# x tiles 2-3 by DMA transpose on the ACT ring, all other loads in order on the SP ring, eight f tiles for tiles 0-1 first

## The chip, the cores and the metric

The kernel runs on one core of one Trainium2 chip. The metric is the device time of one execution in microseconds (us), the median over several executions. TensorE (PE) does the matmuls, VectorE (DVE) and ScalarE (ACT) move and activate what comes out of PSUM, and the SyncE (SP) and ACT sequencers ask for DMA transfers. Each of these two sequencers has a ring of its own, and both rings are served by the same 16 DMA engines. In the profile the SP ring is queue q1 and the ACT ring is q10.

Measured time before: 105.89 us (median of 6 runs in the rounds with the change).

## The reference

```python
# x: (1, 2048, 512)  w1: (512, 1792)  b1: (1792)  w2: (1792, 512), all bf16
h = einsum("bsd,df->bsf", x, w1) + b1
act = h * tanh(softplus(h))              # Mish
out = einsum("bsf,fd->bsd", act, w2)
```

The contraction of the first product runs over D, so x has to arrive with D on the partitions: it must be transposed.

## The kernel before

The 2048 rows of x are worked in four blocks of 512. For each block the 14 "f tiles" of h (128 columns of w1 each) are made by four matmuls of 512 columns (`mm1`), passed through Mish on ACT, and multiplied with w2 (`mm2`). Blocks 1 to 3 get x by DMA transpose. Block 0 cannot wait for that: its four x tiles of 128 rows are loaded plainly and transposed by TensorE.

```python
# loads of before, in order of issue (F0 = 4: f tiles 0-3 come first)
t_xa  = load(sp,  x tile 0)                    # 128 KB
t_w1k = load(act, w1 rows k 0-1, f 0-3)        # 256 KB
t_xb  = load(sp,  x tile 1)
t_w1k+= load(act, w1 rows k 2-3, f 0-3)        # "w1's lower half"
t_xc  = load(sp,  x tiles 2-3)
t_b1  = load(act, b1)
load(sp, w1 f 4-7); load(sp, w1 f 8-13); load(sp, w2)       # 512, 768, 1792 KB
for s in 1..3: load(sp, xT block s, x block s, transpose=True)
... # cut; what PE does in the head:
part_T([0], t_xa)                  # 4 transposes on PE, copies on DVE and ACT
first_mm1([0], by_k(0, 1))
part_T([1], t_xb)
first_mm1([1], by_k(0, 1)); first_mm1([0, 1], by_k(2))
part_T([2, 3], t_xc)               # 8 transposes on PE
first_mm1([0, 1], by_k(3))
first_mm1([2, 3], ...)             # f 0-3 are done for block 0
... # cut: b1 is transposed, Mish of f 0-3
for t in range(F0, FT): mm1(t)     # f 4-13, 512 columns at a time
```

(The first block above is shortened; arguments stand for the slices.)

## Time and profile before

| | before |
|---|---|
| median time | 105.89 us |
| span of the profiled run | 103.9 us |
| PE busy | 97% |
| first full `mm1` (f tile 4) starts | 8.83 us |
| `mm2` of block 0 starts | 17.25 us |

The page of before says what bounds it. The first line gives busy time and share of the span; the rows of digits give busy tenths in 40 slices of 2.6 us; the last two lines are the chain of waits by engine and by line.

```profile
PE 101.1 (97%) x513; PEld 50.0 (48%) x522; DVE 13.0 (12%) x25; ACT 40.4 (39%) x63; POOL 0.6 (1%) x6
...
PE   8999999999999999999999999999999999999992
...
PEclk9999999999999999999999999999999999999999
...
PE 97%; issue 1%; DVE 0%
PE ps L206 46%; PE ps L180 43%; PE ps L151 4%; PE ps L119 2%; PE ps L133 1%; DVE o_sb L210 0%; DVE warm L115 0%; PE ps L226 0%
```

TensorE is the bound from end to end. Only its first 9 us hold anything but full matmuls. The timeline of PE shows them (start, length, what, count, and in brackets the idle time before and what ended it):

```profile
3.15 1.03 PE L151 MATMUL ps<-xT,w_sb 128*128 128x128 bf16 x8
3.98 0.63 PE L133 MATMUL ps<-ident,x_nat 128*128 128x128 bf16 x4
4.61 1.32 PE L151 MATMUL ps<-xT,w_sb 128*128 128x128 bf16 x12
5.77 0.61 PE L133 MATMUL ps<-ident,x_nat 128*128 128x128 bf16 x8
6.22 2.35 PE L151 MATMUL ps<-xT,w_sb 128*128 128x256 bf16 x20
8.50 0.18 PE L226 MATMUL ps<-ident,b_nat 14*128 14x14 bf16 x1
8.83 8.58 PE L180 MATMUL ps<-xT,w_sb 128*128 128x512 bf16 x39 [0.16 <-issue]
17.25 2.97 PE L206 MATMUL ps<-w_sb,a_sb 128*128 128x512 bf16 x12
```

The eight transposes of tiles 2-3 are the line at 5.77; the next work starts 0.45 us later. That is what the change wants to save. In the instructions of this stretch, 128-column matmuls start 107 ns apart until 5.2 us and 56 ns apart afterwards: the TensorE clock is halved until then.

The DMA view of before gives each issue with its size and the time from issue to landing. The two first pieces of w1 go on the ACT ring; the second of them, issued at 0.58 us, lands at 4.76. The transposes are those of blocks 1 to 3.

```profile
w_sb<-in_w_dram SPq DMA_DIRECT2D x1, 1792.0 KB, 12.7
...
w_sb<-in_w_dram ACTq DMA_DIRECT2D x2, 256.0 KB, 3.6
...
xT<-in_x_dram SPq DMA_TRANSPOSE x3, 5.5
```

### The profile page before, as it was taken

Reading aid. Unit: us, or ns where it says so; the run is one execution under the profiler, and the core shown is the slowest. Engines: PE = TensorE matmul, PEld = TensorE weight load, DVE = VectorE, ACT = ScalarE, POOL = GpSimd, SP = SyncE. Lnnn points to the kernel's source line nnn. Section 1 sums busy time; section 2 is a strip of 40 time slices with the busy share of each in tenths; the row PEclk is TensorE's granted clock in tenths of the full one; section 3 lists DMA queues with packets and bytes.
Section 4 is the critical chain, followed back from the end, with each engine's and each line's share of the span. In section 5 each row is a group of like instructions: output and inputs, shape, how many; then the busy total and the mean of one; then the engine's idle time right before and its main releaser. Section 6 shows DMA issues by size and latency. Waiting matters only on the chain.

```text
span 103.9 us, 1168 instructions
## 1 busy us (share of the span) xinstructions
PE 101.1 (97%) x513; PEld 50.0 (48%) x522; DVE 13.0 (12%) x25; ACT 40.4 (39%) x63; POOL 0.6 (1%) x6
## 2 busy tenths in 40 slices
PE   8999999999999999999999999999999999999992
PEld 7895444444444444444444444444444444444462
DVE  0310000112220000022220000022112000011223
ACT  2525997000027777200007777500005777700000
POOL 2000000000000000000000000000000000000000
PEclk9999999999999999999999999999999999999999
DMA  5999996951101000010111000001111000001111
GB/s 169 294 349 376 349 187 149 260 146 50 50 7 43 0 6 0 0 50 14 37 50 50 0 3 6 0 0 50 50 50 50 0 0 0 0 6 50 50 50 51
DMA packets 12561, 7.94 MB, mean 76 GB/s; under 512 B 6796, under 2 KB 12428, under 8 KB 12556
## 3 DMA queue, kind: packets, MB, share of 16 engines
q1 hardware_dynamic: 11984, 7.34, 26.5%
q10 hardware_dynamic: 572, 0.53, 1.5%
q8 instruction: 4, 0.07, 0.3%
q14 instruction: 1, 0.01, 0.0%
HBM read 4.20 MB, written 2.10 MB: 61 GB/s over the span
## 4 chain that ended last, share of the span: by engine, by line
PE 97%; issue 1%; DVE 0%
PE ps L206 46%; PE ps L180 43%; PE ps L151 4%; PE ps L119 2%; PE ps L133 1%; DVE o_sb L210 0%; DVE warm L115 0%; PE ps L226 0%
## 5 line engine op out<-in xcount | busy, mean ns | idle before, releaser
L173 ACT ACTIVATE a_sb<-ps,b_sb 128x512 bf16<-128x512 f32 x56 | 37.5, 691 | 46.3 <-PE ps L180 44.2
L206 PE MATMUL ps<-w_sb,a_sb 128*128 128x512 bf16 (+2 forms) x234 | 48.8, 366 | 0.2
L180 PE MATMUL ps<-xT,w_sb 128*128 128x512 bf16 x203 | 45.1, 379 | 0.4 <-issue 0.2
L206 PEld LDWEIGHTS ps<-w_sb,a_sb 128*128 128x128 bf16 x238 | 22.8, 98 | 25.9
L180 PEld LDWEIGHTS ps<-xT,w_sb 128*128 128x128 bf16 x208 | 20.3, 98 | 24.3
L210 DVE CAST o_sb<-ps 128x512 bf16<-128x512 f32 (+2 forms) x17 | 11.2, 660 | 82.3 <-PE ps L206 82.3
L151 PE MATMUL ps<-xT,w_sb 128*128 128x256 bf16 (+1 forms) x40 | 4.7, 282 | 0.0
L151 PEld LDWEIGHTS ps<-xT,w_sb 128*128 128x128 bf16 x40 | 3.7, 113 | 0.7 <-DVE xT L138 0.3
L119 PE MATMUL ps<-warm 128*128 128x128 bf16 x19 | 2.4, 310 | 0.4 <-DVE warm L115 0.4
L141 ACT ACTIVATE xT<-ps 128x128 bf16<-128x128 bf16 (+1 forms) x6 | 1.6, 311 | 2.1 <-PE ps L133 2.1
L119 PEld LDWEIGHTS ps<-warm 128*128 128x128 bf16 x19 | 2.0, 143 | 0.4 <-DVE warm L115 0.4
L138 DVE COPY xT<-ps 128x128 bf16<-128x128 bf16 (+1 forms) x6 | 1.4, 247 | 4.9 <-PE ps L133 4.9
L111 ACT ACT_TABLE_LOAD x1 | 1.3, 1283 | 1.8 <-issue 1.8
L133 PE MATMUL ps<-ident,x_nat 128*128 128x128 bf16 x16 | 1.8, 263 | 0.0
L133 PEld LDWEIGHTS ps<-ident,x_nat 128*128 128x128 bf16 x16 | 1.3, 118 | 0.3 <-issue 0.2
L227 DVE CAST b_sb<-ps 128x14 f32<-128x14 bf16 x1 | 0.2, 173 | 2.1 <-PE ps L226 2.1
L109 POOL TENSOR_SCALAR_AFFINE_SELECT ident<-ones 128x128 bf16<-128x128 bf16 x1 | 0.3, 295 | 0.1
L107 POOL MEMSET ones<- 128x128 bf16 x1 | 0.2, 205 | 0.0
L226 PEld LDWEIGHTS ps<-ident,b_nat 14*128 14x128 bf16 x1 | 0.1, 90 | 0.2 <-issue 0.2
L115 DVE MEMSET warm<- 128x128 bf16 x1 | 0.2, 165 | 0.2 <-issue 0.2
L226 PE MATMUL ps<-ident,b_nat 14*128 14x14 bf16 x1 | 0.2, 177 | 0.0
L260 POOL MEMSET const-bfloat16-1.0<- 128x1 bf16 x1 | 0.1, 103 | 0.0
(3 smaller groups left out, 0.3 us busy)
## 6 DMA issues: line engine op xcount, KB each, us to landing
out_dram<-o_sb SPq DMA_DIRECT2D x15, 128.0 KB, 1.7
w_sb<-in_w_dram SPq DMA_DIRECT2D x1, 1792.0 KB, 12.7
w_sb<-in_w_dram SPq DMA_DIRECT2D x1, 768.0 KB, 8.2
w_sb<-in_w_dram ACTq DMA_DIRECT2D x2, 256.0 KB, 3.6
w_sb<-in_w_dram SPq DMA_DIRECT2D x1, 512.0 KB, 6.5
x_nat<-in_x_dram SPq DMA_DIRECT2D x2, 128.0 KB, 2.6
x_nat<-in_x_dram SPq DMA_DIRECT2D x1, 256.0 KB, 3.9
out_dram<-o_sb SPq DMA_DIRECT2D x1, 96.0 KB, 1.6
```

What stands on the lines that cost most here:

```text
L109: t_id = pool.mark(pool.eng.affine_select(ident[:, :], ones[:, :], pattern=[[1, P]], compare_op=ALU.is_equal, fill=0.0, base=0, channel_mu ...
L111: act.eng.preload_act_table(ACT.Mish)
L119: nc.tensor.matmul(ps[:, 7, 0:P], warm[:, :], warm[:, :], start=True, stop=True)
L133: tr = nc.tensor.transpose(psk[:, n * P:(n + 1) * P], x_nat[:, j, k * P:(k + 1) * P], ident[:, :])
L138: t = dve.mark(nc.vector.tensor_copy(dst, psk))
L141: t = act.mark(act.eng.activation(dst, psk, ACT.Copy))
L151: mm = nc.tensor.matmul(ps[:, 4 + f, cs], w1_sb[:, k, f * P:(f + 1) * P], xT[:, k, cs], start=(js[0] == 0 and k == 0), stop=(js[-1] == JT ...
L173: t_mish[t] = act.mark(act.eng.activation(a_sb[:, t, :], ps[:, bank1(t), :], ACT.Mish, bias=b1_sb[:, f:f + 1]))
L180: mm = nc.tensor.matmul(ps[:, bank1(t), :], w1_sb[:, k, f * P:(f + 1) * P], xT[:, k, s * SBW:(s + 1) * SBW], start=(k == 0), stop=(k == KT ...
L206: mm = nc.tensor.matmul(ps[:, bank, 0:hi - lo], a_sb[:, t, j * P:(j + 1) * P], w2_sb[:, f, lo:hi], start=(f == 0), stop=(f == FT - 1))
L210: t_bank[bank] = dve.mark(nc.vector.tensor_copy(o_sb[:, i, lo:hi], ps[:, bank, 0:hi - lo]))
L226: dve.wait(pe.mark(nc.tensor.transpose(psb1, b1_nat[:, :], ident[0:FT, 0:FT])))
```

## The change

The intent: let the DMA engines transpose tiles 2-3, so that TensorE is spared eight transposes. To hide the DMA transpose, tiles 0-1 do eight f tiles instead of four before tiles 2-3 are needed. The transpose is asked for on the ACT ring, once w1's lower half (f 0-3, k 2-3) is in; everything else but the small b1 goes on the SP ring in the order in which it is needed. The DMA transposes of blocks 1 to 3 wait for the first one to land. (The Trainium skill, "DMA: Bandwidth & Descriptors", section "Silent corruption: two transposing streams in flight at once", asks for that wait between two rings that transpose; no run here tried it without.)

```diff
+        act.wait(t_b1z)
+        t_b1 = load(act, b1_nat[0:FT, :], ...)
+        act.eng.preload_act_table(ACT.Mish)
+        t_xa = load(sp, x_nat[:, 0, :], x2[0:P, :], "s_xa")
+        t_w1k = [load(sp, w1_sb[:, 0:2, 0:F0 * P], ..., "s_w1k0")] * 2
+        t_xb = load(sp, x_nat[:, 1, :], x2[P:2 * P, :], "s_xb")
+        t_w1k += [load(sp, w1_sb[:, 2:4, 0:F0 * P], ..., "s_w1k2")] * 2
+        act.wait(t_w1k[2])
+        t_xT = [load(act, xT[:, :, 2 * P:SBW], x2[2 * P:SBW, :], "s_xT0", True)]
+        for k in (0, 2):                       # w1 f 4-7, in two pieces
+            t_w1m += [load(sp, ...)] * 2
+        t = load(sp, w1_sb[:, :, 2 * F0 * P:F], ..., "s_w1_8")     # w1 f 8-13
         t_w2 = load(sp, w2_sb[:, :, :], w2v, "s_w2")
+        sp.wait(t_xT[0])
         for s in range(1, NSB): t_xT.append(load(sp, ..., True))
...
-        part_T([2, 3], t_xc)                   # and the ACT half of the copies
+        first_mm1([0, 1], by_k(F0, *range(KT)))
+        first_mm1([2, 3], [(f, k) for f in range(2 * F0) for k in range(KT)])
+        for t in range(2 * F0, FT): mm1(t)
```

(Cut to its core: the old loads, the copies of the transposes, now all on DVE, and the new place of the b1 transpose are left out.)

More of the change, by code (lines that the diff above doesn't have):

```diff
@@ L57, in sb @@
             return es.enter_context(nc.sbuf_tensor(name, shape, t))
-        x_nat = sb("x_nat", [P, JT, D], BF)
+        x_nat = sb("x_nat", [P, 2, D], BF)
         xT = sb("xT", [P, KT, S], BF)
@@ L62, in bass_standalone__dense_activation_mish__prompt_kernel @@
         w2_sb = sb("w2_sb", [P, FT, D], BF)
-        b1_nat = sb("b1_nat", [FT, P], BF)
+        b1_nat = sb("b1_nat", [P, P], BF)
         b1_sb = sb("b1_sb", [P, FT], F32)
@@ L85, in bass_standalone__dense_activation_mish__prompt_kernel @@
         n_pre = len(nc.cur_bb.bb.instructions)
-        x0v = [x2[0:P, :], x2[P:2 * P, :], x2[2 * P:SBW, :].rearrange("(p j) d -> p j d", j=2)]
-        t_xa = load(sp, x_nat[:, 0, :], x0v[0], "s_xa")
-        t_w1k = [load(act, w1_sb[:, 0:2, 0:F0 * P], w1v[:, 0:2, 0:F0 * P], "s_w1k0")] * 2
-        t_xb = load(sp, x_nat[:, 1, :], x0v[1], "s_xb")
-        t_w1k += [load(act, w1_sb[:, 2:4, 0:F0 * P], w1v[:, 2:4, 0:F0 * P], "s_w1k2")] * 2
-        t_xc = load(sp, x_nat[:, 2:4, :], x0v[2], "s_xc")
-        t_b1 = load(act, b1_nat[:, :], b1.rearrange("(j p) -> j p", p=P), "s_b1")
-        t_w1 = {}
-        for a, b in ((4, 8), (8, FT)):
-            t = load(sp, w1_sb[:, :, a * P:b * P], w1v[:, :, a * P:b * P], "s_w1_%d" % a)
-            for f in range(a, b):
-                t_w1[f] = t
+        warm = sb("warm", [P, P], BF)
+        t_warm = dve.mark(nc.vector.memset(warm[:, :], 1.0))
+        t_b1z = dve.mark(nc.vector.memset(b1_nat[:, :], 0.0))
+        act.wait(t_b1z)
+        t_b1 = load(act, b1_nat[0:FT, :], b1.rearrange("(j p) -> j p", p=P), "s_b1")
+        act.eng.preload_act_table(ACT.Mish)
+        t_xa = load(sp, x_nat[:, 0, :], x2[0:P, :], "s_xa")
+        t_w1k = [load(sp, w1_sb[:, 0:2, 0:F0 * P], w1v[:, 0:2, 0:F0 * P], "s_w1k0")] * 2
+        t_xb = load(sp, x_nat[:, 1, :], x2[P:2 * P, :], "s_xb")
+        t_w1k += [load(sp, w1_sb[:, 2:4, 0:F0 * P], w1v[:, 2:4, 0:F0 * P], "s_w1k2")] * 2
+        act.wait(t_w1k[2])
+        t_xT = [load(act, xT[:, :, 2 * P:SBW], x2[2 * P:SBW, :], "s_xT0", True)]
+        t_w1, t_w1m = {}, []
+        for k in (0, 2):
+            t_w1m += [load(sp, w1_sb[:, k:k + 2, F0 * P:2 * F0 * P], w1v[:, k:k + 2, F0 * P:2 * F0 * P], "s_w1m%d" % k)] * 2
+        t = load(sp, w1_sb[:, :, 2 * F0 * P:F], w1v[:, :, 2 * F0 * P:F], "s_w1_8")
+        for f in range(2 * F0, FT):
+            t_w1[f] = t
         t_w2 = load(sp, w2_sb[:, :, :], w2v, "s_w2")
-        t_xT = [None]
+        sp.wait(t_xT[0])
         for s in range(1, NSB):
@@ L110, in bass_standalone__dense_activation_mish__prompt_kernel @@
                                                 fill=0.0, base=0, channel_multiplier=-1))
-        act.eng.preload_act_table(ACT.Mish)
-        warm = sb("warm", [P, P], BF)
-        pe.wait(dve.mark(nc.vector.memset(warm[:, :], 1.0)))
+        pe.wait(t_warm)
         def dummies(n):
@@ L119, in dummies, with part_T @@
                 nc.tensor.matmul(ps[:, 7, 0:P], warm[:, :], warm[:, :], start=True, stop=True)
-        t_cp, t_mm1 = {}, {}
-        n_cp = 0
-        def part_T(js, tok):
-            nonlocal n_cp
-            lo, hi = js[0] * P, (js[-1] + 1) * P
+        t_cp = {}
+        def part_T(j, tok):
             pe.wait(tok)
             for k in range(KT):
-                pe.wait(t_cp.get((js[0] - 1, k)))
-                psk = ps[:, k, 0:(hi - lo) // 2].bitcast(BF)
-                for n, j in enumerate(js):
-                    tr = nc.tensor.transpose(psk[:, n * P:(n + 1) * P], x_nat[:, j, k * P:(k + 1) * P], ident[:, :])
-                t = pe.mark(tr)
-                dst = xT[:, k, lo:hi]
-                if k % 2 == 0:
-                    dve.wait(t)
-                    t = dve.mark(nc.vector.tensor_copy(dst, psk))
-                else:
-                    act.wait(t)
-                    t = act.mark(act.eng.activation(dst, psk, ACT.Copy))
-                for j in js:
-                    t_cp[j, k] = t
+                pe.wait(t_cp.get((j - 1, k)))
+                psk = ps[:, k, 0:P // 2].bitcast(BF)
+                dve.wait(pe.mark(nc.tensor.transpose(psk, x_nat[:, j, k * P:(k + 1) * P], ident[:, :])))
+                t_cp[j, k] = dve.mark(nc.vector.tensor_copy(xT[:, k, j * P:(j + 1) * P], psk))
         def first_mm1(js, fks):
@@ L149, in first_mm1, with by_k @@
             for f, k in fks:
-                pe.wait(t_w1k[k], *[t_cp[j, k] for j in js])
-                mm = nc.tensor.matmul(ps[:, 4 + f, cs], w1_sb[:, k, f * P:(f + 1) * P], xT[:, k, cs],
+                pe.wait((t_w1k if f < F0 else t_w1m)[k])
+                if js[0] == 0 and k == 0:
+                    pe.wait(t_bank.get(bank1(f)))
+                pe.wait(*([t_cp[j, k] for j in js] if js[0] < 2 else t_xT[:1]))
+                mm = nc.tensor.matmul(ps[:, bank1(f), cs], w1_sb[:, k, f * P:(f + 1) * P], xT[:, k, cs],
                                       start=(js[0] == 0 and k == 0), stop=(js[-1] == JT - 1 and k == KT - 1))
                 if js[-1] == JT - 1 and k == KT - 1:
-                    t_mm1[f] = pe.mark(mm)
-        def by_k(*ks):
-            return [(f, k) for k in ks for f in range(F0)]
+                    mish(f, pe.mark(mm))
+        def by_k(f0, *ks):
+            return [(f, k) for k in ks for f in range(f0, f0 + F0)]
         dummies(N_WARM)
         pe.wait(t_id)
-        part_T([0], t_xa)
+        part_T(0, t_xa)
         dummies(N_FILL)
@@ L185, in store @@
             q.wait(tok)
-            rows = o0v[:, i % 2, :] if i in (2, 3) else out2[i * P:(i + 1) * P, :]
-            q.eng.dma_start(rows[:, lo:hi], o_sb[:, i, lo:hi]).then_inc(s_out, 16)
+            q.eng.dma_start(out2[i * P:(i + 1) * P, lo:hi], o_sb[:, i, lo:hi]).then_inc(s_out, 16)
         s_out = sem("s_out")
-        o0v = out2[2 * P:SBW, :].rearrange("(p j) d -> p j d", j=2)
         n_out = 0
@@ L212, in mm2 @@
                 n_out += 1
+        first_mm1([0], by_k(0, 0))
+        part_T(1, t_xb)
         first_mm1([0], by_k(0, 1))
-        part_T([1], t_xb)
-        first_mm1([1], by_k(0, 1))
-        first_mm1([0, 1], by_k(2))
-        part_T([2, 3], t_xc)
-        first_mm1([0, 1], by_k(3))
-        first_mm1([2, 3], by_k(0, 1) + [(f, k) for f in range(F0) for k in (2, 3)])
-        for k in range(KT):
-            t_bank[k] = t_cp[JT - 1, k]
-        pe.wait(t_b1, t_bank[3])
-        psb1 = ps[:, 3, 0:FT // 2].bitcast(BF)
-        dve.wait(pe.mark(nc.tensor.transpose(psb1, b1_nat[:, :], ident[0:FT, 0:FT])))
-        t_bank[3] = t_b1c = dve.mark(nc.vector.tensor_copy(b1_sb[:, :], psb1))
-        for f in range(F0):
-            mish(f, t_mm1[f])
-        for t in range(F0, FT):
+        first_mm1([1], by_k(0, 0, 1))
+        first_mm1([0, 1], by_k(0, 2))
+        pe.wait(t_b1, t_cp[1, 3])
+        psb1 = ps[:, 3, 0:P // 2].bitcast(BF)
+        dve.wait(pe.mark(nc.tensor.transpose(psb1, b1_nat[:, :], ident[:, :])))
+        t_b1c = dve.mark(nc.vector.tensor_copy(b1_sb[:, :], psb1[:, 0:FT]))
+        t_bank[3] = t_b1c
+        first_mm1([0, 1], by_k(0, 3))
+        for k in range(KT - 1):
+            t_bank[k] = t_cp[1, k]
+        first_mm1([0, 1], by_k(F0, *range(KT)))
+        first_mm1([2, 3], [(f, k) for f in range(2 * F0) for k in range(KT)])
+        for t in range(2 * F0, FT):
             mm1(t)
```

## The prediction

> **What bounds the kernel now.** TensorE. The page gives PE 97% busy, and the chain of waits is 97% PE from 0.4 us to the last copy; the timeline shows PE without a gap over 0.2 us. In steady state one 512-column matmul starts every 0.216 us; 448 of them are 96.7 us of the 103.9 us span. What is left is the head. The first full matmul (w1 tile 4) starts at 8.83 us, by when only 16 matmuls' worth (3.45 us) is done: 5.4 us lost to the first loads (x tile 0 lands at 2.15 us, the first w1 piece at 3.11), 16 transposes, the b1 transpose, and a cold clock (starts 107 ns apart for 128 columns until 5.2 us, 56 after). Only the head can gain.
>
> **What the change removes.** The 8 transposes of tiles 2-3 (5.77 to 6.22 us on PE, 0.45 us) and most of the 0.3 us of gaps around the b1 transpose. At most 0.7 us.
>
> **What it adds and moves.** The loads queue on SP in the order in which the engines already served them; w1's first piece is issued at 0.46 instead of 0.12 us, but x tile 0 fills the engines until 1.75 us anyway: landing within 0.2 us of before. All copies go to DVE (four in a row, 0.22 us each); the k-wise order hides them. So, stepping through the new order with the measured intervals: tiles 0-1 of f 0-3 end near 6.3 us, of f 4-7 near 8.1 us. If tiles 2-3 are there, 32 matmuls of 256 columns (109 ns) end at 11.6 us; before reached that point at 12.3: 105.3 us.
>
> **The crux: when tiles 2-3 land.** ACT may issue at about 4.3 us. From the SP transposes (512 rows: issue 2.2 to 3.0 us when not held up, landing 2.2 us after the issue's end, 2048 packets of 256 B at 1100 per us) I estimate for half of one: 1.3 us issue, 2.2 us to landing, so 7.9 us on idle engines. They are not idle: SP has then queued all of w1 and w2, about 3 MB, busy to about 13 us. The Trainium skill (DMA: Bandwidth & Descriptors, "Queues, rings and completion order") says that each engine round-robins between rings, packet by packet. The trace's early order (x0, w1, x1, w1 from two rings, hardly mixed) fits long turns, but also service in order of issue. The first transpose of before, with w2's tail on some engines, needed over 4 us of packets instead of 2, with stretches in which hardly any moved[...]. I expect a landing near 9.6 us (8.3 to 11): TensorE idles about 1.5 us, more than the 0.7 us won. If service is in order of issue (one chance in five), it lands after w2, near 15 us, and costs 7 us and perhaps the clock.
>
> **Predicted time** 106.8 us, range 105.4 to 112.5. Faster by over 2%: 0.01; within 2%: 0.60; slower by over 2%: 0.39.
>
> **What would show it.** PE timeline: tiles 0-1 of eight f tiles ending near 8.1 us, then one gap of 1 to 3 us released by the transpose; DMA issues: that transpose 4 to 6 us from issue to landing instead of 3.5; matmuls from tile 8 on unchanged at 0.216 us; no new wait for w1 f 4-7 before 8 us, none at w2, the later transposes or the stores.
>
> **What would make it wrong.** The transpose landing before 8.1 us (then 105.3), or held behind w2; w1 f 4-7 late (the DMA rate dipped to 130 GB/s near 4.7 us); a long gap slowing the clock again.

## The result and the profile after

| | before | after |
|---|---|---|
| median of 6 runs | 105.89 us | 114.73 us (113.48 to 115.01) |
| ratio, with 95% interval | 1 | 1.082 (1.076 to 1.088) |
| span of the profiled run | 103.9 us | 111.9 us |
| PE busy | 97% | 91% |

Ratios here are the mean time of one kernel's fast runs over that of the other's in the same rounds, so not quite the ratio of the medians. All six runs of after count as fast; one of before's six, 107.2 us, lies 1.6% above its fastest, over the 1.5% at which a run is called slow, and the others lie between 105.55 and 106.0. The change costs 8%, more than the whole predicted range allows. The profiled run of after is the fastest of its six (113.48 us; the other spans are 112.6 to 113.4 us), so what follows explains that run, and up to 1.5 us of the loss in the other runs stands in no trace. The page of after, the same parts as shown of before:

```profile
PE 101.7 (91%) x521; PEld 51.4 (46%) x530; DVE 12.9 (11%) x28; ACT 39.0 (35%) x57; POOL 0.6 (1%) x6
...
PE   8781059999999999999999999999999999999993
...
PEclk9999557999999999999999999999999999999999
...
PE 84%; DMA 12%; SPq 1%; issue 1%; DVE 0%
PE ps L199 43%; PE ps L175 37%; DMA xT<-in_x_dram 8%; PE ps L146 4%; DMA w_sb<-in_w_dram 4%; SPq L82 1%; DVE o_sb L203 0%
```

Two things are new: a hole in PE's row, from the fourth slice into the sixth, and a halved TensorE clock (the 5s) that sets in during it and outlasts it. The chain of waits puts 8% of the span on the DMA into xT. The PE timeline of after:

```profile
4.25 0.87 PE L146 MATMUL ps<-xT,w_sb 128*128 128x128 bf16 x12
5.98 0.61 PE L146 MATMUL ps<-xT,w_sb 128*128 128x256 bf16 x4 [0.85 <-DMA w_sb<-in_w_dram]
6.42 0.22 PE L215 MATMUL ps<-ident,b_nat 128*128 128x128 bf16 x1
6.48 2.35 PE L146 MATMUL ps<-xT,w_sb 128*128 128x256 bf16 x20
15.18 5.01 PE L146 MATMUL ps<-xT,w_sb 128*128 128x256 bf16 x32 [6.36 <-DMA xT<-in_x_dram]
20.24 5.13 PE L175 MATMUL ps<-xT,w_sb 128*128 128x512 bf16 x23
25.21 1.03 PE L199 MATMUL ps<-w_sb,a_sb 128*128 128x512 bf16 x4
```

There is a wait of 0.85 us for w1's lower half, and one of 6.36 us for the transpose. After it the 32 matmuls of tiles 2-3 take 5.01 us instead of the 3.5 us that 109 ns each would make. From 20.24 us on, everything runs as before: `mm2` of block 0 starts at 25.21 us, 7.96 us later than before, and the span is 8.0 us longer. So the whole loss of this run lies in the first 20 us.

The DMA view of after, in two short stretches around the issues of w1's lower half and of the transpose, shows the times from issue to landing. The transpose is issued at 5.95 us and takes 9.2 us:

```profile
w_sb<-in_w_dram SPq DMA_DIRECT2D x1, 256.0 KB, 4.5
...
xT<-in_x_dram ACTq DMA_TRANSPOSE x1, 9.2
```

The trace's records of single DMA packets split these 9.2 us. The transpose is 1024 packets of 256 bytes (64 per engine). The first runs at 10.03 us, 4.1 us after the issue; the last at 14.44 us. While they run, the same view for the stretch from 12 to 14 us (packets, MB, share of the 16 engines' time) shows the two rings taking turns, one packet each:

```profile
q1 hardware_dynamic: 564, 0.58, 81.1%
q10 hardware_dynamic: 566, 0.14, 31.8%
```

q1's packets are w2's rows of 1024 bytes. Equal counts would fit longer turns too, but the start times do not: 558 times in these 2 us a q1 packet starts 14 ns after one of q10, where chance would give some 160. One pair of packets costs an engine 56.5 ns (16 engines x 2000 ns / 566).

So there were two questions for experiments. First, what held the transpose back for 4.1 us before its first packet? Second, how much of the loss is the wait, the alternation, the clock, and the late w1? My theory at that point, "order of issue": transfers start in the order in which they were asked for, whichever ring they are on, so the transpose stands behind w1 f 8-13 and w2. The rival, "slow to start": a DMA transpose on the ACT ring itself takes some 4 us before its first packet.

### The profile page after: what moved, and what is told of

Same layout as the page of the kernel before. It is cut to its first block, busy times and chain, and to the rows that moved or that the text cites. A ratio compares the mean times of both kernels' runs of the same rounds, so it can differ in the third digit from the quotient of the medians.

```text
span 111.9 us, 1183 instructions
## 1 busy us (share of the span) xinstructions
PE 101.7 (91%) x521; PEld 51.4 (46%) x530; DVE 12.9 (11%) x28; ACT 39.0 (35%) x57; POOL 0.6 (1%) x6
## 4 chain that ended last, share of the span: by engine, by line
PE 84%; DMA 12%; SPq 1%; issue 1%; DVE 0%
PE ps L199 43%; PE ps L175 37%; DMA xT<-in_x_dram 8%; PE ps L146 4%; DMA w_sb<-in_w_dram 4%; SPq L82 1%; DVE o_sb L203 0%
## 5 line engine op out<-in xcount | busy, mean ns | idle before, releaser
L175 PE MATMUL ps<-xT,w_sb 128*128 128x512 bf16 x188 | 41.7, 379 | 0.2
L175 PEld LDWEIGHTS ps<-xT,w_sb 128*128 128x128 bf16 x192 | 18.8, 98 | 22.4
L146 PE MATMUL ps<-xT,w_sb 128*128 128x256 bf16 (+1 forms) x72 | 9.3, 293 | 7.5 <-DMA xT<-in_x_dram 6.4
L146 PEld LDWEIGHTS ps<-xT,w_sb 128*128 128x128 bf16 x72 | 7.1, 111 | 9.4 <-DMA xT<-in_x_dram 6.6
L135 DVE COPY xT<-ps 128x128 bf16<-128x128 bf16 x8 | 1.2, 216 | 3.2 <-PE ps L134 3.2
L134 PE MATMUL ps<-ident,x_nat 128*128 128x128 bf16 x8 | 1.2, 307 | 0.0
L134 PEld LDWEIGHTS ps<-ident,x_nat 128*128 128x128 bf16 x8 | 0.8, 136 | 0.2 <-issue 0.2
```

Source lines behind the costliest of these rows:

```text
L134: dve.wait(pe.mark(nc.tensor.transpose(psk, x_nat[:, j, k * P:(k + 1) * P], ident[:, :])))
L135: t_cp[j, k] = dve.mark(nc.vector.tensor_copy(xT[:, k, j * P:(j + 1) * P], psk))
L146: mm = nc.tensor.matmul(ps[:, bank1(f), cs], w1_sb[:, k, f * P:(f + 1) * P], xT[:, k, cs], start=(js[0] == 0 and k == 0), stop=(js[-1] == ...
L175: mm = nc.tensor.matmul(ps[:, bank1(t), :], w1_sb[:, k, f * P:(f + 1) * P], xT[:, k, s * SBW:(s + 1) * SBW], start=(k == 0), stop=(k == KT ...
```

## The experiments

Runs with "one look" have one time, so their state is unknown; their differences to before are read only where they are over 1%. The profile of each decides.

### a. w2 asked for only after tiles 2-3 are in

```diff
+        sp.wait(t_xT[0])
         t_w2 = load(sp, w2_sb[:, :, :], w2v, "s_w2")
-        sp.wait(t_xT[0])
```

> The SP ring waits for x tiles 2-3 before it issues w2 (not before w1's f 8-13). Theory 'order of issue': descriptors for the two rings are made in the order in which they were asked for, so the transpose only stands behind w1 f 8-13; its first packets start about 7.5 to 8.5 us instead of 10.2, they no longer alternate with w2, and it lands near 9.5 to 10 us; TensorE waits 1 to 1.5 us, the clock stays up, time near 107.5. Rival 'slow to start': the ACT transpose itself needs some 4 us from issue to its first packet whatever else is queued; first packets still near 10.2 us, landing near 11.5 to 12, wait near 3 us, time near 109. In both, w2 lands near 16 us, just in time.

Measured: 107.9 us, one look (before: 105.47). The first packet of the transpose came at 8.06 us, 1.7 us after the issue at 6.34, and it landed at 10.64. From the DMA view around the issue:

```profile
xT<-in_x_dram ACTq DMA_TRANSPOSE x1, 4.3
```

And from its PE timeline:

```profile
10.69 3.67 PE L146 MATMUL ps<-xT,w_sb 128*128 128x256 bf16 x32 [1.47 <-DMA xT<-in_x_dram]
```

Taking w2 out of the queue halved the time to landing. "Slow to start" falls. The clock stayed up, and TensorE's wait for the transpose was 1.47 us. One part of the expectation was a miss: w2, expected near 16 us, landed at 19.63, and the first `mm2` (19.68 us) waited some 0.3 us for it.

### b. w1 f 8-13 and w2 asked for only after tiles 2-3 are in

```diff
+        sp.wait(t_xT[0])
         t = load(sp, w1_sb[:, :, 2 * F0 * P:F], ..., "s_w1_8")
...
-        sp.wait(t_xT[0])
```

> The SP ring waits for x tiles 2-3 before w1's f 8-13 and w2. Theory 'order of issue': nothing stands before the transpose but w1 f 4-7; first packets within about 1 us of its issue (near 7 us), landing near 8.7 to 9; then w1 f 8-13 lands near 12 and w2 near 17, perhaps a short wait for each; time near 107. Rival 'slow to start': first packets still near 10.2 us, landing near 11.5, then w1 f 8-13 and w2 late too (14.5 and 20 us), time over 110.

Measured: 108.53 us, one look. First packet at 7.11 us, 1.37 us after the issue; landing at 9.08. The DMA view of this run, at the issue and then from 7.1 to 8.6 us, where q10 has the engines to itself:

```profile
xT<-in_x_dram ACTq DMA_TRANSPOSE x1, 3.3
...
q10 hardware_dynamic: 1053, 0.26, 89.1%
```

Alone, the transpose takes 3.3 us from issue to landing and 1.5 us of packets, against 9.2 and 4.4 us in the change. (My estimate from the transposes of before had been 3.5 us.) But now w1 f 8-13, issued at 9.10 us, comes late: TensorE waits 2.26 us for it.

```profile
15.05 5.34 PE L175 MATMUL ps<-xT,w_sb 128*128 128x512 bf16 x24 [2.26 <-DMA w_sb<-in_w_dram]
```

The prediction of "near 107" for the time missed this; its landing near 12 us became 14.9.

### c. The transpose asked for at once

```diff
-        act.wait(t_w1k[2])
```

> ACT issues the transpose at about 1.1 us without the wait for w1's lower half; all else as in the change. 'Order of issue': only x tiles 0-1 and w1 k 0-1 are ahead; first packets near 3 us, mixed with w1's pieces, landing near 6 to 7 us, before TensorE needs it at 8.7; w1's k 2-3 lands up to 1 us later; no wait for the transpose, time 105.5 to 107. 'Slow to start': first packets near 5.5 us, landing near 8 to 10 us, time 106 to 108.

Measured: 109.82 us, one look. The first packets came at 2.92 us and it landed at 7.93, before TensorE needed it, as "order of issue" says. The time was a miss all the same. The transpose now takes turns with the loads that TensorE waits for: w1's lower half lands at 7.57 us instead of 5.93. The PE timeline of this run:

```profile
7.62 1.04 PE L145 MATMUL ps<-xT,w_sb 128*128 128x256 bf16 x4 [1.26 <-DMA w_sb<-in_w_dram]
...
8.55 8.02 PE L145 MATMUL ps<-xT,w_sb 128*128 128x256 bf16 x52
```

Those 52 matmuls take 8.02 us where 109 ns each would be 5.7: the trace records the full clock only from 13.0 us on. That the clock opened so late because TensorE kept stopping is my reading; no run isolates it here.

### d. A plain load in the transpose's place

The same 256 KB, into the same place, at the same moment and on the same ring, but not transposed. Its results are wrong on purpose.

```diff
-        t_xT = [load(act, xT[:, :, 2 * P:SBW], x2[2 * P:SBW, :], "s_xT0", True)]
+        t_xT = [load(act, xT[:, :, 2 * P:SBW],
+                     x2[2 * P:SBW, :].rearrange("(p a) (b c) -> p (a b) c", a=2, b=2), "s_xT0")]
```

> A plain load of the same 256 KB into the same place of xT on the ACT ring at the same moment (wrong values on purpose: not transposed). 'Order of issue': a plain load is held back as the transpose was; first packets 2 us or more after its issue, landing at 10 us or later. Rival 'it is the transpose': first packets 1.0 to 1.4 us after issue, as for the loads at the start, landing near 9 us, TensorE waits under 1 us, time near 106.5.

Measured: 113.51 us, one look. First packet 4.08 us after the issue, exactly as for the transpose; landing 7.8 us after it. The DMA view at the issue and from 11 to 12 us:

```profile
xT<-in_x_dram ACTq DMA_DIRECT2D x1, 256.0 KB, 7.8
...
q1 hardware_dynamic: 221, 0.23, 71.3%
q10 hardware_dynamic: 218, 0.11, 40.3%
```

So neither the delay nor the alternation belongs to the transpose: with w1 f 8-13 and w2 queued on the first ring, a plain load that comes late to the second one gets both as well. The transpose's packets took longer, 4.4 us against 3.1, which fits its 64 turns per engine instead of 32 (its packets have 256 bytes, the plain load's 512).

### e. The transpose in order on the SP ring

```diff
-        act.wait(t_w1k[2])
-        t_xT = [load(act, ..., "s_xT0", True)]
...
+        t_xT = [load(sp, ..., "s_xT0", True)]        # after w1 f 4-7, before w1 f 8-13
         t = load(sp, w1_sb[:, :, 2 * F0 * P:F], ..., "s_w1_8")
...
-        sp.wait(t_xT[0])
```

> The change with its transpose of x tiles 2-3 moved to the SP ring, in order between w1's f 4-7 and f 8-13, without the wait for w1's lower half. Theory 'order of issue, then packet by packet with the other ring': now nothing stands before it but what is needed earlier and nothing alternates with it; its 1024 packets run at about 18 ns each from about 6.9 us, landing 8.5 to 9.2 us; TensorE waits 0 to 0.5 us; w1's lower half still lands near 5.9 us; time 105.9 to 106.8, near before. If instead the transpose is slow beside any queued load whatever the ring: landing after 11 us and over 108.

Measured, 3 rounds: 105.58 us (before 105.66 in the same rounds), ratio 1.001 (0.997 to 1.005). The transpose landed at 8.29 us; PE timeline:

```profile
6.22 5.84 PE L144 MATMUL ps<-xT,w_sb 128*128 128x256 bf16 x52
11.89 5.34 PE L173 MATMUL ps<-xT,w_sb 128*128 128x512 bf16 x24
17.18 1.04 PE L197 MATMUL ps<-w_sb,a_sb 128*128 128x512 bf16 x4
```

All 52 matmuls run through without a wait, and `mm2` starts at 17.18 us (before: 17.25). The whole 8% is gone. This edit changes three things together (the ring, the place in the order, the wait for w1), so it shows what to do rather than which of the three counts most; a, b and c are the parts of it. Note that the transpose is issued at 2.92 us and needs 5.4 us to land, longer than in b. As I read it, that does not matter, because what it stands behind is only what TensorE needs earlier, and what it would compete with comes after it.

It does not beat before: as I read this profile, the eight transposes saved (0.45 us) are given back by a later first matmul (3.35 us instead of 3.15), a short wait for w1's lower half, and a clock that opened at 5.98 us in this profile instead of 5.2.

### f and k. Was it the ring that made w1's lower half late?

In f, on top of e, w1's two first pieces are back on the ACT ring as in before. In k only the lower half is, after b1.

```diff
 # f_w1_on_act
-        t_w1k = [load(sp, ..., "s_w1k0")] * 2
+        t_w1k = [load(act, ..., "s_w1k0")] * 2
-        t_w1k += [load(sp, ..., "s_w1k2")] * 2
+        t_w1k += [load(act, ..., "s_w1k2")] * 2
 # k_w1k2_act: only "s_w1k2", issued on ACT between b1 and the table load
```

> e_sp_order, with w1's first two pieces (f 0-3) back on the ACT ring, issued there at 0.1 and 0.6 us as in before. Theory 'the move to the SP ring made w1's lower half late' (4.76 us before, 5.7 to 6.3 in every run since): it lands near 4.8 us again, TensorE's wait of 0.9 us before k 2 goes, tiles 0-1 of eight f tiles end near 8.1 us, the transpose lands near 8.5 to 9; time 105.2 to 106.2. Rival 'the slow stretch of the loads near 3 to 4.5 us comes whatever the ring': the lower half still lands near 5.7 us or later, and the time is that of e_sp_order within 0.3 us.

> e_sp_order with only w1's lower half of f 0-3 moved to the ACT ring, asked for there after b1 at about 1.1 us (SP asked at 1.42; in f_w1_on_act ACT asked at 0.58 and it landed at 4.85). If the ring is what made it late: landing near 4.8 us. If it is when it is asked for, or what has been asked for before it: landing 5.2 to 5.5 us. The time is within 0.5 us of e_sp_order in both.

Measured: it landed at 4.85 us in f and at 4.86 us in k, although k issues it at 1.13 us and f at 0.58. On the SP ring, issued at 1.42 or 1.43 us, it landed between 5.16 and 6.32 us in the ten other kernels that leave it there and do not start the transpose early (after, a, b, d, e, g2, h, i, j, l). That is 0.3 to 1.5 us earlier, but k also asks 0.3 us earlier: from issue to landing it takes 3.73 us in k and 4.26 in f, against 3.73 (i) to 4.89 us (a) on the SP ring, in nine of those ten over 4.0. So an effect of the ring itself is possible but not shown. In the packet records the SP ring's loads run slowly from about 3 to 4.5 us (in after 65 to 81 packets in each half microsecond, where from 5 us on it is 150 or more), and in f and k the two rings together do not (over 145); why is open. The time did not follow: f took 105.65 us (ratio 1.001, 0.997 to 1.006), k 105.66 us in one look. In both profiles the clock opened only at 6.1 and 6.5 us, so that TensorE, now without a wait, was slow instead. When the clock first opens varies from profile to profile, from 3.67 us (j) to 6.49 (k) in those that record it before TensorE's long wait, with c (13.0 us) as the exception; differences of some tenths of a us in this stretch are partly luck.

### g2. Keeping the clock up during the wait

```diff
+        for _ in range(52):       # zeros, into columns that are still to be written
+            nc.tensor.matmul(ps[:, bank1(0), 2 * P:4 * P], zero[:, 0:P], zero[:, :], start=False, stop=False)
         first_mm1([2, 3], ...)
```

(Cut: `zero` is a tile that is set to 0 at the start.)

> The change with 52 matmuls of zeros (256 columns, 5.7 us) put in front of the wait for x tiles 2-3, adding nothing to the results. If the halved clock after the wait is due to TensorE's idle stretch, the granted clock stays at 1.0, the 32 matmuls after the wait take 3.5 us instead of 4.9, the landing near 15.1 us is unchanged, and the time falls by 1.2 to 1.5 us, to about 113.3. If the low clock has another cause, the time is that of the change, 114.7.

Measured, 3 rounds: 113.5 us (113.38 to 113.93), ratio to before 1.076 (1.072 to 1.079), against 1.082 for the change; the medians differ by 1.2 us. They come from different rounds, so the verdict rests on the profile. The stretches view, first for after, then for g2 (start and end, length, PE busy and its matmuls, granted clock, DMA share, GB/s):

```profile
8.60:11.10 2.50, 0.23 (x3) 1.00 1.13 344
11.10:15.20 4.10, 0.02 (x1) 0.50 0.98 309
15.20:18.00 2.80, 2.80 (x14) 0.51 0.79 53
18.00:20.30 2.30, 2.25 (x21) 1.00 1.03 229
```

```profile
8.60:11.10 2.50, 2.50 (x26) 1.00 1.08 347
11.10:16.40 5.30, 3.41 (x32) 1.00 1.12 235
16.40:20.00 3.60, 3.60 (x33) 1.00 0.71 156
```

In after the clock halves 2.5 us after TensorE stops and opens again 2.8 us after it resumes; in g2 it never drops. (g2's profile records no change of clock at all, so its 1.00 proves nothing by itself; the 32 matmuls after the wait start 109 ns apart, and that is the full clock.) In g2's profile the transpose happened to land 1.2 us later (16.36 us), and still f tile 8 started at 19.91 us, 0.3 us before after's 20.24. The halved clock is thus a consequence of the idle wait. In after's profile it costs 1.35 us of the 8: the 32 matmuls start over 4.84 us instead of 3.49. The Trainium skill, "TensorE: Matmul & The Clock Gate", section "Part 1: The HAM clock gate", says that the clock halves after an idle window of about 3.4 us and opens after a busy one. The low stretch fits this: 6.83 us, two such windows, in all six profiles in which the clock dropped (after, d, h, i, j, l). The delays fit it less well: 2.5 us from the stop is shorter than a whole window, and over the six they run from 2.4 (i) to 5.1 us (j).

### h, i, j, l. What holds the newcomer back?

The hold was the part of the theory still open. In h only half of w2 is in the queue before the transpose. In i all of it is, but as two loads. In j a tiny load stands behind w2. In l, w1 f 8-13 and w2 are asked for in rows of 512 bytes.

```diff
 # h_w2_half: first half of w2 before sp.wait(t_xT[0]), second half after it
 # i_w2_two:  both halves before it, as two loads
 # j_tiny:    after w2
+        t_tiny = load(sp, tiny[:, :], x2[0:P, 0:8], "s_tiny")       # 2 KB
 # l_small:   w1 f 8-13 as three loads of 256 columns, w2 as two of 256
```

> The change with w2 loaded in two halves, the second one issued only after x tiles 2-3 are in. Theory 'the transpose is held until everything asked for earlier has been handed to the engines[...]': with half of w2 gone from the queue (56 of 112 packets per engine) there is hardly any hold; first packets near 7.5 us instead of 10.2; but they alternate one by one with w1 f 8-13 (65 ns a packet) and then w2, so it still takes some 5 us and lands near 12.5; wait near 3.8 us, time near 110. Rival 'behind all that is queued': starts only as w2's first half ends, near 11 us, landing near 12.5 at 18 ns a packet.

> The change with w2 asked for as two loads of half the size, both before the transpose is asked for, so that one more load stands before it and the bytes are the same. Where halving what stood in the queue (h_w2_half) changed the transpose's start little, the new theory is: a DMA starts some 0.9 us after the last but one asked for before it, on either ring, has been moved. It then starts after the first half of w2, near 12.5 to 13 us instead of 10.1, and lands near 15.5 to 16.5. Rival 'w1 f 8-13 is what holds it' (or the bytes or packets queued): it starts near 10.1 us as in the change.

> The change with one tiny load (128 x 16 B) asked for on the SP ring after w2. Theory 'the last but one before it must have been moved': the last but one is now w2 itself, so the transpose starts near 15.5 us, 5 us later than in the change, alternates with nothing, and lands near 17.5; the time is near 117. Rival 'held by w1 f 8-13, by bytes or by packets queued': the tiny load changes nothing, start near 10.1 us, landing near 15.1.

> The change with w1 f 8-13 and w2 asked for in 512-byte rows (five loads, same bytes) instead of rows of 1536 and 1024 bytes. In the six kernels with w2 queued, 68 to 79 packets per engine of the SP ring went between the transpose's issue and its first packet (4.1 to 4.4 us), however w2 was cut. Theory 'a stock of a fixed number of packets already handed to each engine goes first, then the rings take turns one packet each': again 68 to 80 packets, now of about 30 ns, so the first packet comes about 3 us after the issue, and each turn costs 18 + 30 ns instead of 18 + 46, 3.1 us in all: landing near 12.5 us instead of 15.1, time near 111 to 112. Rival 'a fixed amount of bytes, or a fixed time': first packet again 4.1 us or more after the issue, with 110 packets or more in between, landing 14 us or later.

All times are one look, issue to first packet read from the packet records. (In l's look, before took 107.3 us on that chip instead of some 105.5, so its time is not compared; its packets are.) "Packets first" are those of the SP ring, per engine, between the two.

| | time, us | issue to first packet, us | packets first | issue to landing, us |
|---|---|---|---|---|
| after (6 runs) | 114.73 | 4.08 | 74 | 9.2 |
| h, half of w2 | 112.4 | 4.29 | 79 | 7.3 |
| i, w2 as two loads | 113.64 | 4.38 | 68 | 10.1 |
| j, tiny load behind w2 | 114.7 | 4.37 | 73 | 9.6 |
| l, 512-byte rows | 113.43 | 3.39 | 119 | 8.9 |
| a, w1 f 8-13 alone | 107.9 | 1.72 | 26 | 4.3 |
| b, neither | 108.53 | 1.37 | 13 | 3.3 |

My first version of "order of issue" said that the transpose waits until everything asked for earlier has been handed over, so h should have started near 7.5 us. It started at 10.0: a miss. The next version, "the last load but one must have been moved", falls with i (9.6 us instead of 12.5 or later) and j (9.9 instead of 15.5). The rival named for i and j, that w1 f 8-13 alone is what holds it, falls with a, where w1 f 8-13 was queued and the first packet came after 1.72 us. What stands is a stock: once much is queued, a fixed lot of work goes first, about 4.1 to 4.4 us from the issue, however w2 is cut, and then the rings alternate. With half-size rows the stock is neither the same number of packets (119 instead of about 74), nor of the same length in time (3.4 instead of 4.1 us), nor, by the packet records, the same number of bytes (65 KB per engine instead of 90 in after). So what fixes its size is not settled. That it was a stock of packets already handed to the engines is my reading, not shown.

j has one more hint: SP needed 4.92 us to issue the tiny load, as the timeline of the SP sequencer shows, where w2 had needed 0.51; I read this as something that had filled up by then:

```profile
2.93 1.02 SPq L82 DMA_DIRECT2D w_sb<-in_w_dram  x2
3.99 4.92 SPq L82 DMA_DIRECT2D tiny<-in_x_dram  x1
```

l bears out the alternation. Its DMA view from 12 to 13 us:

```profile
q1 hardware_dynamic: 414, 0.21, 73.2%
q10 hardware_dynamic: 415, 0.11, 47.9%
```

Again one for one, and a pair now costs 38.6 ns per engine (16 x 1000 / 415) instead of 56.5, as one expects when the other ring's packets are half as long. Its landing (14.66 us) still missed the 12.5 expected, because both rings slowed from about 10.0 us and nearly stood still from 10.4 to 11.4 us, with single packets taking up to 1.8 us. Why is open; see the last section.

## Why the prediction was wrong

What held:

- The bound and the most that could be won were right. e, f and k show the full version of the idea without its DMA trouble: within 0.5% of before. The 0.7 us at most were eaten by small losses in the head.
- "The crux: when tiles 2-3 land" was the crux: one long gap on PE, ended by the transpose, and nothing lost from tile 8 on.
- The estimate for idle engines, 3.5 us from issue to landing, measured 3.3 (b).
- The clock was named as a danger of a long gap.

What failed is the step "I expect a landing near 9.6 us (8.3 to 11): TensorE idles about 1.5 us". It landed at 15.14 us. Term by term:

| term of the landing at 15.14 us | predicted, us | measured, us | shown by |
|---|---|---|---|
| ACT may issue at | 4.3 | 5.95 | w1's lower half lands at 5.93 on the SP ring; 4.85 on ACT (f, k) |
| issue to landing on idle engines | 3.5 | 3.3 | b |
| of which issue to first packet | | 1.37 | b |
| added by queues and sharing | 1.7 | 5.9 (9.2 - 3.3) | a, b, d |
| of which the hold before the first packet | | 2.7 (4.08 - 1.37) | after, b |
| of which packets slower than alone, beside w2 | | 2.9 (4.4 - 1.5) | after, b |

Put in order of time: issue at 5.95, 1.37 to a start on idle engines, 2.7 of hold, 4.4 of packets, 0.7 from the last packet to the landing, 15.1 us in all. Of the 4.4 us of packets, 64 turns of 56.5 ns are 3.6; in the rest the turns set in gradually (4, 14 and 31 packets of the transpose in the first three stretches of 0.2 us) and both rings slowed near 11 us. Three things were sized wrong:

1. "The loads queue on SP in the order in which the engines already served them ... landing within 0.2 us of before." w1's first piece kept to that nearly (3.38 against 3.11 us), but the lower half, which opens the gate, came 1.2 us later than before. I checked only the first piece, and the 4.3 us that I wrote down was earlier even than before's 4.76.
2. I gave queueing and sharing 1.7 us together, taking "long turns" and "service in order of issue" as alternatives. It was a bit of both, one after the other: first a hold of 2.7 us, then turns of a single packet. With packets of 256 bytes against 1024, such turns leave it little: the transpose got a fifth of the bytes (0.14 of 0.72 MB between 12 and 14 us) while it was the only transfer that anything waited for. The early part of before's trace, which I read for turns, shows long stretches of one ring although the other had been asked too (from 2.0 to 2.5 us, 159 packets of ACT's and 21 of SP's); it does not show when that gives way to turns.
3. The clock, 1.35 us, was counted only in the unlikely case.

The sum for the time at which f tile 8 starts: I expected 11.6 + 1.5 = 13.1 us. It was 20.24: 0.6 us from the later end of tiles 0-1 (8.66 instead of 8.1), 5.0 from the longer wait (6.5 instead of 1.5), 1.35 from the clock, 0.2 from a small gap. The 20% case of the prediction, landing near 15 us and a cost of 7 us and perhaps the clock, gave the right figure for the wrong reason: the transpose did not wait for w2 to finish; its last packet ran beside w2's.

The upper end of the range, 112.5 us, had the 15 us landing but left out its clock penalty. With 1.35 us for it, it would have reached the profiled run (113.48) but still not the median, 114.73.

## What to carry to other kernels

In this kernel, the transfer that the critical path waits for did best in the same ring as the bulk loads, after what is needed earlier and before what is needed later (e). The second ring was no fast lane once about 2.5 MB (w1 f 8-13 and w2) were queued on the first one: the newcomer was first held back for some 4 us and then got every other packet, and as its packets were small (the transpose's have 256 bytes) it got a fifth of the bytes. A gate that starts a transfer "when the loads before it are in" does not keep later loads, already queued, from getting ahead of it; and the idle gap of 6.5 us on TensorE cost 1.35 us more in clock.

## What the Trainium skill lacked or had wrong

- "DMA: Bandwidth & Descriptors", section "Queues, rings and completion order": it says that each engine takes the rings in turn at packet granularity, draining a whole packet of about 9 to 17 descriptors before switching. Once both rings were active the records show turns of single row-sized packets (564 to 566 in 2 us, 558 pairs of them 14 ns apart). The page gives no time for a newcomer that is held first: 4.1 to 4.4 us from issue to first packet with w1 f 8-13 and w2 queued in large rows, 1.7 us without w2 (a), 1.4 us with neither (b).
- The same page, section "Rules for kernel authors", says of the mix that a transpose next to ordinary DMAs "needs nothing". That is said of correct data, and results were right here; of time it says nothing, and the transpose's packets took 4.4 us beside w2 instead of 1.5 alone.
- The same page, section "Issuing engines are not separate DMA queues", has the choice of issuing engine save only issue time. Here w1's lower half, asked for at 1.13 us on the ACT ring, landed 3.73 us later, and asked for at 1.43 us on the SP ring, 3.73 to 4.89 us later (over 4.0 in nine of ten kernels): a hint that the ring matters, not shown.
- No page has the standstills seen beside transposes: for 1.0 us (l, 10.4 to 11.4 us) or 1.4 us (g2, 13.6 to 15.0 us) hardly any packet of either ring moved, and before has one too (15.5 to 16.7 us). In g2 and before it came soon after a 16 KB instruction fetch began (13.29 and 14.94 us); in l there was no such fetch.
- "TensorE: Matmul & The Clock Gate", section "Part 1: The HAM clock gate", had the length of the clock's window right (low for 6.83 us, twice 3.4, in six profiles). Its "after an idle window" is too coarse for a single wait: the clock halved 2.4 to 5.1 us after TensorE stopped.
- On reading a profile, no page says that the granted clock has no record before its first change: the stretch view prints 1.00 for before's first 5 us, where the starts of matmuls are 107 ns apart instead of 56. In b and g2 no change is recorded at all, although in b the starts go from 107 to 57 ns apart near 6.6 us.
